# The last two products of a three-stage kernel in thirds of 512 tokens instead of halves of 768

## The chip, the core and the metric

The kernel runs on one core of a Trainium2 chip. The metric is the device time of one execution in microseconds (us). Matrix products run on TensorE (PE; its weight loads are shown apart as PEld), and the other engines are VectorE (DVE), ScalarE (ACT), GpSimd (POOL) and SyncE (SP), which here only issues DMAs. Products are summed in PSUM, which has eight banks of 128 partitions by 512 float32 each.

## What is computed

Three stages follow each other: an attention with a window and block summaries (2 batches, 8 heads, 768 positions, head size 64), a feed-forward layer of width 1024 with a normalisation, and a second feed-forward layer of width 2048. The change is about the last one, and about when its weights are made ready.

```
x = attention(q, k, v)                    # 1536 tokens x 512
h = x @ w_in                              # 1536 x 1024
ln = normalise(h * softmax(h)) * g_ln
x = ln @ w_out                            # 1536 x 512
h = x @ w_in2                             # 1536 x 2048
g = where(h > 0, h, exp(min(h, 0)) - 1)
out = g @ w_out2                          # 1536 x 512
```

## The kernel before

**Three products for one.** Each float32 product of the two feed-forward layers is made of three matmuls (`mm3x`, lines 98 to 100): every operand is split into a rounded part "hi" and the rest "lo", and hi·hi, hi·lo and lo·hi are summed in PSUM. The attention's own small products are plain float32.

**The weights** come as 64-bit floats and are turned into hi and lo on the chip by `convert` (lines 106 to 121), 128x512 words at a time. One conversion is a DMA of 512 KB into a staging slot, ACT's absolute value (L113), POOL's clamp (L114), three DVE steps on the bits (L115, L116, L117), ACT's copy that rounds to hi (L120) and DVE's subtraction that leaves lo (L95). A slot is free again once L117 has read it. There are 48 conversions: 8 of w_in, 8 of w_out, 16 of w_in2 (called w3) and 16 of w_out2 (called w4).

**The first phase** (lines 345 to 433) holds the attention, the first layer and w_in and w_out's conversions. It runs in ticks of one 128-token tile and half a product each. Its last part, after the ticks, holds the rest of the first layer's second product (`y_ps`), whose result goes to the tiles `y`, here two of 768 tokens each.

**The tiles `y` lend their space** until the results come: their rows hold the values that `sum_v` adds up (six DMAs of 128x512), and their 1024-word pieces are the staging slots. With two tiles there are three slots in each: `early` is the six of both, `stage[1]` serves the first w3 weights and `stage[0]`, with one tile of its own, the rest, once `split_y` has turned y[0] into hi and lo (`y_hl`).

**The second phase** (lines 436 to 500) takes the tokens in two halves of TC = 768. For each of the 16 pieces f of the hidden width, `ffn2_in` makes h in two matmul groups of 384 columns (2 x 12 matmuls; tiles h, then m, then the hi and lo of g in `g_hl`): ACT's relu and exp (L447, L448), a DVE step (L449), ACT's copy to hi (L450) and DVE's subtraction to lo (L95). `ffn2_out` then adds piece f into six output sums `o_ps` of 128 tokens each (6 x 3 matmuls of 512 columns). Four of these sums have banks of their own (`pso`), and two take half of the four banks (`psb`) that h is written to. `more_w(2)` at each f converts two more weights while any are left; six w3 and w4 are converted or under way before the second phase begins.

**What sets the order.** SP's DMAs keep the order of the program. The instructions of the other engines are put in an order, engine by engine, by a scheduler when the kernel is built, and each engine then runs its own list strictly in that order (TensorE's is by hand in the last two pieces).

Of the kernel before, what the change touches and what calls it, by code (L numbers as in the profile page):

```python
# [9 lines left out]
F32 = mybir.dt.float32  # L10
# [19 lines left out]
NTOK = B * S  # L30
NJ = NTOK // 128
TB = 384
TC = 768
KD, KF1, KF2 = DM // 128, F1 // 128, F2 // 128
NEG = -1.0e9
LEAD = 6
NBUF = 3
NG = 4


def f32_of(bits):
# [8 lines left out]
def tile_kernel(ctx: ExitStack, tc: tile.TileContext, qd, kT, v, w_in, w_out, g_ln, w_in2, w_out2,  # L50
# [46 lines left out]
    def mm3x(ps, l, ls, r, rs, first, last):  # L97
        nc.tensor.matmul(ps, lhsT=l[0][ls], rhs=r[0][rs], start=first, stop=False)  # L98
        nc.tensor.matmul(ps, lhsT=l[0][ls], rhs=r[1][rs], start=False, stop=False)  # L99
        nc.tensor.matmul(ps, lhsT=l[1][ls], rhs=r[0][rs], start=False, stop=last)  # L100
# [19 lines left out]
        nc.scalar.activation(hi, x, AF.Copy)  # L120
        lo_of(lo, x, hi)

    early = stage[0] + stage[1]

    def load_w_in(n, k):
        cs = slice(n * 512, (n + 1) * 512)
# [22 lines left out]
    def sum_v(b):  # L149
        pst = psb.tile([128, DM], F32, tag="b", name="vs_ps")  # L150
        for i in range(S // 128):
            vt = rows[1][i]
            nc.sync.dma_start(vt, v[b, PAD + i * 128:PAD + (i + 1) * 128, :])
            c0 = NB - i * 4
            nc.tensor.matmul(pst, lhsT=avg[:, c0:c0 + 128], rhs=vt, start=i == 0, stop=i == S // 128 - 1)
        vsum[b] = p_at.tile([128, DM], F32, tag="vsum", name="vsum", bufs=1)
        nc.scalar.activation(vsum[b][WIN:KW, :], pst[WIN:KW, :], AF.Copy)
# [102 lines left out]
    def ffn1_out(i, d, k):  # L260
        if k == 0:
            ys[d] = psb.tile([128, 512], F32, tag="b", name="y_ps")
        mm3x(ys[d][:, :TB], w_out_hl[k], (al, slice(d * 128, (d + 1) * 128)), lnT_of(i), (al, k, al),
             k == 0, k == KF1 - 1)
        if k == KF1 - 1:
            nc.scalar.activation(y[i // 2][:, d, i % 2 * TB:(i % 2 + 1) * TB], ys[d][:, :TB], AF.Copy)

    w3, w4, yhl = [], [], {}

    def bits():  # L270
        state["late"] += 1
        if not yhl:
            return stage[1][state["late"] % 3]
        i = state["late"] % 4
        return stage[0][i] if i < 3 else p_w3.tile([128, KD, 256], I32, name="bits", tag="bits", bufs=1)

    def load_w3():
        f = len(w3)
# [31 lines left out]
            elif len(w4) < KF2:  # L310
                load_w4()

    def split_y(i, n):
        yhl[i, n] = [p_y.tile([128, KD, TB], F32R, tag=f"y{n}{c}", name="y_hl", bufs=1) for c in range(2)]
        for k in range(0, KD, 2):
            src = y[i][:, k:k + 2, n * TB:(n + 1) * TB]
            hi, lo = (t[:, k:k + 2, :] for t in yhl[i, n])
            nc.scalar.activation(hi, src, AF.Copy)
            lo_of(lo, src, hi)

# [70 lines left out]
    for t, (j, n) in enumerate(ticks):  # L391
        s_n, p_n, x_n = t + LEAD, t + LEAD - 2, t + LEAD - 3
        if t == 0:
            sum_v(1)
        elif t == 1:
            load_k(1)
        elif t == 3:
            sum_k(1)
        if x_n < NU and t:
            load_v(x_n)  # L400
        if s_n < NU:
            for u in (s_n + 1, s_n):
                if u < NU and u not in q_bd:
                    load_q(u)
            attn_s(s_n)
        mm_in(j, n)
        if p_n < NU:
            attn_p(p_n)
        for f, *args in after[t]:
            f(*args)  # L410
        if x_n < NU:
            attn_x(x_n)
        more(converts.get(t, 0))
        if t in (13, 15):
            load_w3()
        if x_n == NU - 1:
            p_at.release()
            p_w3 = ctx.enter_context(tc.tile_pool(name="p_w3", bufs=1, side="left", reuse_waits="tile"))
            lnT_last = [p_w3.tile([128, KF1, TB], F32R, tag=f"lnT{c}", name="lnT") for c in range(2)]
    p_in.release()  # L420
    p_y = ctx.enter_context(tc.tile_pool(name="p_y", bufs=1, side="right", reuse_waits="tile"))
    for d in range(KD):
        mm_out(NJ // 3 - 2, d)
        if d == 2:
            split_y(0, 0)
            split_y(0, 1)
        if d < 3:
            tr(NJ - 3 + d)
    for d in range(KD):
# [8 lines left out]
    ghl = [p_w.tile([128, NG, TC], F32R, tag=f"lnT{c}", name="g_hl") for c in range(2)]  # L438

    def ffn2_in(i, f):  # L440
        for n in range(TC // TB):
            gh, gl = (a[:, f % NG, n * TB:(n + 1) * TB] for a in ghl)
            m = p_y.tile([128, TB], F32, tag="m", name="m", bufs=3)
            h2 = psb.tile([128, 512], F32, tag="b", name="h2")[:, :TB]
            for k in range(KD):
                mm3x(h2, w3[f], (al, k, al), yhl[i, n], (al, k, al), k == 0, k == KD - 1)
            nc.scalar.activation(m, h2, AF.Relu, scale=-1.0)  # L447
            nc.scalar.activation(m, m, AF.Exp, scale=-1.0)  # L448
            nc.vector.scalar_tensor_tensor(m, m, -1.0, h2, op0=ALU.add, op1=ALU.max)  # L449
            nc.scalar.activation(gh, m, AF.Copy)  # L450
            lo_of(gl, m, gh)
            if f == KF2 - 1 and i + 1 < NTOK // TC:
                split_y(i + 1, n)

    def ffn2_out(ops, t, f):
        mm3x(ops[t], [a[:, f % NG, :] for a in ghl], (al, slice(t * 128, (t + 1) * 128)), w4[f], (al,),
# [18 lines left out]
        nc.sync.dma_start(out[r0:r0 + 128, :], o)  # L475

    for i in range(NTOK // TC):
        ops = [(pso if t < 4 else psb).tile([128, DM], F32, tag="o" if t < 4 else "b", name="o_ps")
               for t in range(NTT)]
        end = i == NTOK // TC - 1  # L480

        for f in range(KF2 - 2 if end else KF2):
# [71 lines left out]
```

## Time and profile before

| | us |
|---|---|
| median of 3 runs | 505.76 (505.55 to 505.81) |
| the profiled execution | 510.05 |
| its span, first to last instruction | 508.3 |
| TensorE busy in the span | 482.9 (95%) |
| DVE busy | 292.2 (57%) |
| ACT busy | 269.9 (53%) |

The profiled execution is 4.29 us above the median of the runs, and 1.75 us of it lie outside the span. Matmuls are pipelined: a matmul's record is longer than the step from its start to the next one's start, so a product is costed by the starts of a long row of matmuls and not by the mean length of one. The same holds, less strongly, for DVE and ACT. "Idle before" names the engine or DMA that ended a wait.

### The profile page before, as it was taken

The numbers are of one execution on the slowest core, as the hardware profiler recorded it, in microseconds if no ns is written. First come the engines' busy times: TensorE is split into PE (matmuls) and PEld (weight loads), VectorE is DVE, ScalarE is ACT, GpSimd is POOL, SyncE is SP. The second block draws the span as 40 slices with busy tenths as digits, with TensorE's granted clock in tenths as the row PEclk, the third lists the DMA queues.
The fourth block names the chain that finished last, engine by engine and source line by source line (L and its number), as shares of the span: only waits on it lengthen the run. The fifth ranks groups of instructions, "written<-read, shape, count | busy, mean of one in ns | idle before, by whom it ended". The sixth has DMA issues, their size and how long they took to land.

```text
span 508.3 us, 7746 instructions
## 1 busy us (share of the span) xinstructions
PE 482.9 (95%) x2808; PEld 425.3 (84%) x2808; DVE 292.2 (57%) x714; ACT 269.9 (53%) x634; POOL 136.3 (27%) x216
## 2 busy tenths in 40 slices
PE   0888999899999999999999999999999999999997
PEld 0564877688888898999889999999998999999895
DVE  2688899697557126899999982222542323232331
ACT  1674898685657235766777763424452424242441
POOL 1877579589323111322132600000000000000000
PEclk9989999999999999999999999999999999999999
DMA  8967662261301010556455500000030000000003
GB/s 289 334 216 278 204 217 92 77 212 59 114 17 33 17 41 1 166 171 202 142 190 165 166 0 2 1 1 0 1 124 1 0 1 0 1 0 1 1 1 125
DMA packets 24567, 46.58 MB, mean 92 GB/s; under 512 B 2256, under 2 KB 11088, under 8 KB 24528
## 3 DMA queue, kind: packets, MB, share of 16 engines
q1 hardware_dynamic: 24528, 46.08, 28.1%
q8 instruction: 22, 0.36, 0.3%
q14 instruction: 17, 0.14, 0.1%
HBM read 42.93 MB, written 3.15 MB: 91 GB/s over the span
## 4 chain that ended last, share of the span: by engine, by line
PE 72%; DVE 12%; DMA 8%; ACT 3%; issue 2%; SPq 1%; POOL 1%; ACTq 0%; DVEq 0%
PE h L98 11%; PE h L100 11%; PE h L99 11%; PE o_ps L100 9%; PE o_ps L98 9%; PE o_ps L99 9%; DMA y<-in_w_out 4%; PE s_ps L178 3%; DVE conv L116 3%; DMA q_bd<-in_qd 3%; PE y_ps L98 2%; PE y_ps L100 2%; DVE conv L117 2%; PE y_ps L99 2%; PE x_ps L214 2%
## 5 line engine op out<-in xcount | busy, mean ns | idle before, releaser
L449 DVE SCALAR_TENSOR_TENSOR m<-m,h 128x384 f32<-128x384 f32 x64 | 35.2, 551 | 100.6 <-ACT m L448 100.6
L98 PE MATMUL h<-y_hl,w 128*128 128x384 f32 x256 | 86.2, 337 | 0.0
L100 PE MATMUL h<-y_hl,w 128*128 128x384 f32 x256 | 86.2, 337 | 0.0
L99 PE MATMUL h<-y_hl,w 128*128 128x384 f32 x256 | 86.2, 337 | 0.0
L447 ACT ACTIVATE m<-h 128x384 f32<-128x384 f32 x64 | 31.2, 487 | 84.4 <-PE h L100 84.3
L98 PE MATMUL o_ps<-w,g_hl 128*128 128x512 f32 x192 | 75.5, 393 | 0.1
L99 PE MATMUL o_ps<-w,g_hl 128*128 128x512 f32 x192 | 75.3, 392 | 0.0
L100 PE MATMUL o_ps<-w,g_hl 128*128 128x512 f32 x192 | 74.0, 392 | 0.0
L114 POOL TENSOR_SCALAR conv<-conv 128x512 f32<-128x512 f32 x48 | 38.2, 798 | 70.8 <-ACT conv L113 69.6
L192 POOL TENSOR_SCALAR sm<-sm,st 128x120 f32<-128x120 f32 x96 | 47.9, 518 | 23.1 <-DVE st L190 20.7
L95 DVE TENSOR_TENSOR g_hl<-m,g_hl 128x384 fp32r<-128x384 f32 x64 | 37.1, 580 | 27.3 <-ACT g_hl L450 27.2
L450 ACT ACTIVATE g_hl<-m 128x384 fp32r<-128x384 f32 x64 | 33.5, 524 | 33.9 <-DVE m L449 33.9
L99 PEld LDWEIGHTS h<-y_hl,w 128*128 128x128 f32 x256 | 48.0, 188 | 1.6
L98 PEld LDWEIGHTS h<-y_hl,w 128*128 128x128 f32 x256 | 48.0, 187 | 1.6
L100 PEld LDWEIGHTS h<-y_hl,w 128*128 128x128 f32 x256 | 48.0, 187 | 0.1
L178 PE MATMUL s_ps<-kw,q_bd 128*128 128x120 f32 x192 | 29.6, 301 | 15.5 <-DMA q_bd<-in_qd 14.0
L113 ACT ACTIVATE conv<-y 128x512 f32<-128x512 f32 x40 | 27.2, 679 | 32.1 <-DMA y<-in_w_in 11.4
L98 PE MATMUL y_ps<-lnT,w_out 128*128 128x384 f32 x128 | 43.8, 342 | 0.0
L99 PE MATMUL y_ps<-lnT,w_out 128*128 128x384 f32 x128 | 43.1, 337 | 0.0
L100 PE MATMUL y_ps<-lnT,w_out 128*128 128x384 f32 x128 | 42.8, 337 | 0.0
L100 PEld LDWEIGHTS o_ps<-w,g_hl 128*128 128x128 f32 x192 | 36.0, 188 | 7.8
L98 PEld LDWEIGHTS o_ps<-w,g_hl 128*128 128x128 f32 x192 | 36.0, 188 | 7.0 <-ACT g_hl L450 0.5
(77 smaller groups left out, 924.6 us busy)
## 6 DMA issues: line engine op xcount, KB each, us to landing
y<-in_w_out SPq DMA_DIRECT2D x23, 512.0 KB, 3.8
y<-in_w_in SPq DMA_DIRECT2D x17, 512.0 KB, 5.5
q_bd<-in_qd SPq DMA_DIRECT2D x24, 256.0 KB, 4.9
vw<-in_v SPq DMA_DIRECT2D x24, 192.0 KB, 4.1
bits<-in_w_in SPq DMA_DIRECT2D x7, 512.0 KB, 3.7
k_sb<-in_kT SPq DMA_DIRECT2D x8, 400.0 KB, 5.7
y<-in_v SPq DMA_DIRECT2D x12, 256.0 KB, 4.4
out<-y SPq DMA_DIRECT2D x11, 256.0 KB, 2.3
```

The costliest lines, as they stand in the source:

```text
L95: nc.vector.tensor_tensor(out_, x, hi.bitcast(F32), op=ALU.subtract)
L98: nc.tensor.matmul(ps, lhsT=l[0][ls], rhs=r[0][rs], start=first, stop=False)
L99: nc.tensor.matmul(ps, lhsT=l[0][ls], rhs=r[1][rs], start=False, stop=False)
L100: nc.tensor.matmul(ps, lhsT=l[1][ls], rhs=r[0][rs], start=False, stop=last)
L113: nc.scalar.activation(x, high.bitcast(F32), AF.Abs)
L114: nc.gpsimd.tensor_scalar(x, x, F64_HUGE, F64_TINY, op0=ALU.min, op1=ALU.max)
L116: nc.vector.scalar_tensor_tensor(a, high, -0x40000000, a, op0=ALU.bitwise_and, op1=ALU.bitwise_or)
L178: nc.tensor.matmul(sps[:, p, 0:KW], lhsT=q_bd[n][:, p, :], rhs=kw[:, p, :], start=True, stop=True)
L192: nc.gpsimd.tensor_scalar(sm[:, p, :], sm[:, p, :], ri[:, p:p + 1], 1.0, op0=ALU.mult, op1=ALU.mult)
L447: nc.scalar.activation(m, h2, AF.Relu, scale=-1.0)
L449: nc.vector.scalar_tensor_tensor(m, m, -1.0, h2, op0=ALU.add, op1=ALU.max)
L450: nc.scalar.activation(gh, m, AF.Copy)
```

## The change

The second phase takes the tokens in three thirds of 512. `ffn2_in` makes h in one matmul group of 512 columns. The output sums are four and all lie in banks of their own, so h has the other four banks. `g_hl` holds six pieces f instead of four (in the same space). `split_y` turns a whole third into hi and lo.

With three tiles `y` of 512 tokens there are two slots in each. `early` is again six slots, but the rows that `sum_v` fills now cover slots 2, 3 and 4 instead of 3, 4 and 5. The first w3 weights go through the two slots of `stage[2]`. Eight of them are begun in the ticks 13, 15 and 17 to 22, instead of two in 13 and 15. Later weights take two slots of `stage[0]` and two tiles `bits`, instead of three and one.

```diff
-TC = 768
+TC = 512
-NG = 4
+NG = 6
...
-    early = stage[0] + stage[1]
+    early = stage[0] + stage[1] + stage[2]
+    v_rows = rows[1] + rows[2]
...
-            vt = rows[1][i]
+            vt = v_rows[i]
...
-            nc.scalar.activation(y[i // 2][:, d, i % 2 * TB:(i % 2 + 1) * TB], ys[d][:, :TB], AF.Copy)
+
+            t0 = i * TB
+            while t0 < (i + 1) * TB:
+                t1 = min((t0 // TC + 1) * TC, (i + 1) * TB)
+                nc.scalar.activation(y[t0 // TC][:, d, t0 % TC:t0 % TC + t1 - t0],
+                                     ys[d][:, t0 - i * TB:t1 - i * TB], AF.Copy)
+                t0 = t1
...
         if not yhl:
-            return stage[1][state["late"] % 3]
+            return stage[2][state["late"] % 2]
         i = state["late"] % 4
-        return stage[0][i] if i < 3 else p_w3.tile([128, KD, 256], I32, name="bits", tag="bits", bufs=1)
+        return stage[0][i] if i < 2 else p_y.tile([128, KD, 256], I32, name="bits", tag="bits", bufs=2)
...
-    def split_y(i, n):
-        yhl[i, n] = [p_y.tile([128, KD, TB], F32R, tag=f"y{n}{c}", name="y_hl", bufs=1) for c in range(2)]
+    def split_y(i):
+        yhl[i] = [p_y.tile([128, KD, TC], F32R, tag=f"y{c}", name="y_hl", bufs=1) for c in range(2)]
...
-        if t in (13, 15):
+        if t in (13, 15, 17, 18, 19, 20, 21, 22):
             load_w3()
...
-        for n in range(TC // TB):
-            gh, gl = (a[:, f % NG, n * TB:(n + 1) * TB] for a in ghl)
-            m = p_y.tile([128, TB], F32, tag="m", name="m", bufs=3)
-            h2 = psb.tile([128, 512], F32, tag="b", name="h2")[:, :TB]
-            for k in range(KD):
-                mm3x(h2, w3[f], (al, k, al), yhl[i, n], (al, k, al), k == 0, k == KD - 1)
...
+        gh, gl = (a[:, f % NG, :] for a in ghl)
+        m = p_y.tile([128, TC], F32, tag="m", name="m", bufs=3)
+        h2 = psb.tile([128, TC], F32, tag="b", name="h2")
+        for k in range(KD):
+            mm3x(h2, w3[f], (al, k, al), yhl[i], (al, k, al), k == 0, k == KD - 1)
...
-        ops = [(pso if t < 4 else psb).tile([128, DM], F32, tag="o" if t < 4 else "b", name="o_ps")
-               for t in range(NTT)]
+        ops = [pso.tile([128, DM], F32, tag="o", name="o_ps") for t in range(NTT)]
```

**Where instructions move.** The order is shown at three places. In the names, y_65 is y[0], y_66 is y[1] and y_67 is y[2]; a name w with a number is a weight's hi or lo; conv is the tile that a conversion works in.

SP in the first 30 us, where weights and the values for the first `sum_v` are fetched, before:

```order
L153 DMA y_66<-in_v 128x512 x6
L107 DMA y_65<-in_w_in 128x1024
L107 DMA y_66<-in_w_in 128x1024
L161 DMA q_bd<-in_qd 128x512
L165 DMA vw_102<-in_v 96x512
...
L107 DMA y_66<-in_w_in 128x1024 x2
L107 DMA y_65<-in_w_in 128x1024
```

and in the change:

```order
L154 DMA y_66<-in_v 128x512 x4
L154 DMA y_67<-in_v 128x512 x2
L107 DMA y_66<-in_w_in 128x1024 x2
L162 DMA q_bd<-in_qd 128x512
L166 DMA vw_103<-in_v 96x512
...
L107 DMA y_67<-in_w_in 128x1024 x2
L107 DMA y_65<-in_w_in 128x1024
```

Both of the two w_in loads behind the six value loads now go to rows that the values have just filled, where before the first went to a slot that no value touches.

DVE at the first pieces of the second phase, from the first m on, before:

```order
L449 SCALAR_TENSOR_TENSOR m<-m,h_2524 128x384
L115 TENSOR_SCALAR conv<-conv 128x512
L116 SCALAR_TENSOR_TENSOR conv<-bits,conv 128x512
L95 TENSOR_TENSOR w_2722<-conv,w_2722 128x512
L449 SCALAR_TENSOR_TENSOR m<-m,h_2543 128x384
L117 SCALAR_TENSOR_TENSOR conv<-bits,conv 128x512
L95 TENSOR_TENSOR g_hl<-m,g_hl 128x384
L115 TENSOR_SCALAR conv<-conv 128x512
L449 SCALAR_TENSOR_TENSOR m<-m,h_2582 128x384
```

and in the change:

```order
L454 SCALAR_TENSOR_TENSOR m<-m,h_2584 128x512
L115 TENSOR_SCALAR conv<-conv 128x512
L95 TENSOR_TENSOR w_2663<-conv,w_2663 128x512
L116 SCALAR_TENSOR_TENSOR conv<-bits,conv 128x512
L95 TENSOR_TENSOR g_hl<-m,g_hl 128x512
L117 SCALAR_TENSOR_TENSOR conv<-bits,conv 128x512
L115 TENSOR_SCALAR conv<-conv 128x512
L454 SCALAR_TENSOR_TENSOR m<-m,h_2624 128x512
```

From the first m to the g of piece 8 the change has, on DVE, the rows of 14 conversions (the subtraction of the last one just behind) and nine m and nine g of 512 columns.

TensorE at the third output piece (f = 2), before:

```order
L98 MATMUL o_ps<-w_2480,g_hl 128x512
L100 MATMUL o_ps<-w_2480,g_hl 128x512 x2
L98 MATMUL h_2677<-y_hl,w_2_2372 128x384
L99 MATMUL h_2677<-y_hl,w_2_2372 128x384
L100 MATMUL h_2677<-y_hl,w_2_2372 128x384
```

and in the change:

```order
L98 MATMUL o_ps<-w_2504,g_hl 128x512
L99 MATMUL o_ps<-w_2504,g_hl 128x512
L98 MATMUL h_2778<-y_hl,w_2_1897 128x512
L100 MATMUL o_ps<-w_2504,g_hl 128x512 x4
L99 MATMUL h_2778<-y_hl,w_2_1897 128x512
L100 MATMUL h_2778<-y_hl,w_2_1897 128x512
```

The eight matmuls of an output piece that need only g's hi stand first, and the four that need its lo behind them. In the change the h of the pieces 0 to 2 and nine of the 12 matmuls of piece 3 stand ahead of the first output matmul. Ahead of the first L100 of the output pieces 4, 7 and 8 stand 137, 204 and 230 matmuls of the second phase.

## Rows read from the trace of the kernel before

**Rows 1.** The page: busy time, share of the span, instructions of each engine.

```profile
PE 482.9 (95%) x2808; PEld 425.3 (84%) x2808; DVE 292.2 (57%) x714; ACT 269.9 (53%) x634; POOL 136.3 (27%) x216
```

**Rows 2.** Busy time by stretches, in us (instructions), clock, DMA share, GB/s.

```profile
core 0: us, PE busy (x) PEld busy (x) DVE busy (x) ACT busy (x) POOL busy (x), PEclk, DMA share, GB/s
...
240.00:260.00 20.00, 19.93 (x102) 17.95 (x102) 19.90 (x36) 15.27 (x31) 4.41 (x6) 1.00 0.56 177
...
300.00:320.00 20.00, 20.00 (x104) 18.39 (x103) 7.09 (x13) 7.96 (x16) 0.00 (x0) 1.00 0.00 1
```

**Rows 3.** TensorE in order of time: start, length, instruction; ends of rows of matmuls.

```profile
55.40 0.39 PE L98 MATMUL h<-w_in,xT 128*128 128x512 f32 x1
...
59.53 0.39 PE L98 MATMUL h<-w_in,xT 128*128 128x512 f32 x1
...
404.51 0.40 PE L98 MATMUL o_ps<-w,g_hl 128*128 128x512 f32 x1
...
408.72 0.34 PE L98 MATMUL h<-y_hl,w 128*128 128x384 f32 x1
...
475.47 0.34 PE L98 MATMUL h<-y_hl,w 128*128 128x384 f32 x1
...
479.67 0.40 PE L98 MATMUL o_ps<-w,g_hl 128*128 128x512 f32 x1
...
483.76 0.34 PE L98 MATMUL h<-y_hl,w 128*128 128x384 f32 x1
```

**Rows 4.** TensorE in order of time: the second phase's first matmul.

```profile
237.00 0.33 PE L98 MATMUL h<-y_hl,w 128*128 128x384 f32 x1
```

**Rows 5.** DVE by line and shape, 222 to 298 us: count, busy, mean ns.

```profile
L95 DVE TENSOR_TENSOR w<-conv,w 128x512 fp32r<-128x512 f32 x25 | 17.0, 680 | 0.0
L116 DVE SCALAR_TENSOR_TENSOR conv<-y,conv 128x512 int32<-128x512 int32 x18 | 14.0, 777 | 0.2
L117 DVE SCALAR_TENSOR_TENSOR conv<-y,conv 128x512 int32<-128x512 int32 x19 | 13.8, 728 | 0.1
L115 DVE TENSOR_SCALAR conv<-conv 128x512 int32<-128x512 int32 x24 | 12.6, 527 | 0.5 <-POOL conv L114 0.5
L95 DVE TENSOR_TENSOR g_hl<-m,g_hl 128x384 fp32r<-128x384 f32 x14 | 9.2, 660 | 0.0
L449 DVE SCALAR_TENSOR_TENSOR m<-m,h 128x384 f32<-128x384 f32 x15 | 8.1, 541 | 0.0
```

**Rows 6.** DVE in order of time: two L115, three conversions apart, none waiting.

```profile
232.69 0.42 DVE L115 TENSOR_SCALAR conv<-conv 128x512 int32<-128x512 int32 x1
...
240.38 0.42 DVE L115 TENSOR_SCALAR conv<-conv 128x512 int32<-128x512 int32 x1
```

**Rows 7.** ACT and DVE by line and shape, from 200 us on: count, busy, mean ns.

```profile
L448 ACT ACTIVATE m<-m 128x384 f32<-128x384 f32 x64 | 33.6, 524 | 1.8
...
L447 ACT ACTIVATE m<-h 128x384 f32<-128x384 f32 x64 | 31.2, 487 | 84.4 <-PE h L100 84.3
...
L95 DVE TENSOR_TENSOR y_hl<-y,y_hl 128x768 fp32r<-128x768 f32 x8 | 7.2, 954 | 4.7 <-ACT y_hl L318 4.7
L318 ACT ACTIVATE y_hl<-y 128x768 fp32r<-128x768 f32 x8 | 6.2, 835 | 0.3 <-PE h L100 0.3
```

**Rows 8.** SP's DMA issues in the first 60 us (a length includes waits inside).

```profile
13.22 4.26 SPq L107 DMA_DIRECT2D y<-in_w_in  x2
17.52 0.43 SPq L161 DMA_DIRECT2D q_bd<-in_qd  x1
...
33.00 8.69 SPq L153 DMA_DIRECT2D y<-in_v  x6
```

**Rows 9.** TensorE in the first 60 us: two waits for q_bd.

```profile
24.47 1.20 PE L178 MATMUL s_ps<-kw,q_bd 128*128 128x120 f32 x8 [1.23 <-DMA q_bd<-in_qd]
...
46.90 1.12 PE L178 MATMUL s_ps<-kw,q_bd 128*128 128x120 f32 x8 [1.10 <-DMA q_bd<-in_qd]
```

**Rows 10.** DVE in the first 60 us: the slots of w_in's loads 4 and 5 read.

```profile
36.93 0.73 DVE L117 SCALAR_TENSOR_TENSOR conv<-y,conv 128x512 int32<-128x512 int32 x1
...
39.84 0.98 DVE L117 SCALAR_TENSOR_TENSOR conv<-y,conv 128x512 int32<-128x512 int32 x1
```

More of the change, by code (lines that the diff above doesn't have):

```diff
@@ L311, in more_w @@
                 load_w4()
-    def split_y(i, n):
-        yhl[i, n] = [p_y.tile([128, KD, TB], F32R, tag=f"y{n}{c}", name="y_hl", bufs=1) for c in range(2)]
+    def split_y(i):
+        yhl[i] = [p_y.tile([128, KD, TC], F32R, tag=f"y{c}", name="y_hl", bufs=1) for c in range(2)]
         for k in range(0, KD, 2):
-            src = y[i][:, k:k + 2, n * TB:(n + 1) * TB]
-            hi, lo = (t[:, k:k + 2, :] for t in yhl[i, n])
+            src = y[i][:, k:k + 2, :]
+            hi, lo = (t[:, k:k + 2, :] for t in yhl[i])
             nc.scalar.activation(hi, src, AF.Copy)
@@ L424, in tile_kernel @@
         if d == 2:
-            split_y(0, 0)
-            split_y(0, 1)
+            split_y(0)
         if d < 3:
@@ L440, in ffn2_in @@
     def ffn2_in(i, f):
-        for n in range(TC // TB):
-            gh, gl = (a[:, f % NG, n * TB:(n + 1) * TB] for a in ghl)
-            m = p_y.tile([128, TB], F32, tag="m", name="m", bufs=3)
-            h2 = psb.tile([128, 512], F32, tag="b", name="h2")[:, :TB]
-            for k in range(KD):
-                mm3x(h2, w3[f], (al, k, al), yhl[i, n], (al, k, al), k == 0, k == KD - 1)
[L447 to L453, printed above, removed]
+        gh, gl = (a[:, f % NG, :] for a in ghl)
[3 more added lines that the diff above has]
+            mm3x(h2, w3[f], (al, k, al), yhl[i], (al, k, al), k == 0, k == KD - 1)
+        nc.scalar.activation(m, h2, AF.Relu, scale=-1.0)
+        nc.scalar.activation(m, m, AF.Exp, scale=-1.0)
+        nc.vector.scalar_tensor_tensor(m, m, -1.0, h2, op0=ALU.add, op1=ALU.max)
+        nc.scalar.activation(gh, m, AF.Copy)
+        lo_of(gl, m, gh)
+        if f == KF2 - 1 and i + 1 < NTOK // TC:
+            split_y(i + 1)
     def ffn2_out(ops, t, f):
```

## The prediction, made before the changed kernel ran

> **What bounds the kernel now.** The page comes first: TensorE is busy for 482.9 of 508.3 us, far above DVE and ACT [rows 1]. A share of the whole can hide stages, so the stretches come next. In 240 to 260 us TensorE and DVE are both full (19.93 and 19.90 us of 20), in 300 to 320 us TensorE is full and DVE is at 7.09 us; the granted clock is 1.00 in both [rows 2]. The chain of waits names DVE's conversions ahead of the first output matmul, but there the two engines run side by side, and TensorE does not wait. So the second phase lasts as long as its matmuls' steps take, provided that DVE keeps up in its first 60 us. The third thing to read is therefore the step of a matmul, from starts in order of time, since records overlap: 24 matmuls of 384 columns from 475.47 to 479.67 step by 175.0 ns; 18 of 512 columns from 479.67 to 483.76 step by 227.2 ns, and 18 others from 404.51 to 408.72 by 233.9 ns; 18 of w_in with 512 columns (55.40 to 59.53) by 229.4 ns [rows 3].
>
> **The wider first product.** Before, h takes 2 halves x 16 pieces x 24 = 768 matmuls of 384 columns. Now it takes 3 x 16 x 12 = 576 of 512. The columns are the same (294,912), so what can be saved is only what a matmul costs apart from its columns, 192 times. Between 175.0 ns at 384 and 227.2 to 233.9 ns at 512 lie 52.2 to 58.9 ns for 128 columns. If the step is a fixed part and a part for each column, the fixed part is 18.4 ns at one end and nothing at the other. Before: 768 x 175.0 = 134.4 us. Now, by the fastest row, 576 x 227.2 = 130.9 (a gain of 3.5); by the slowest, 134.7 (a loss of 0.3); by w_in's row 576 x 229.4 = 132.1, a gain of 2.3 us. I take 2.5 us (229 ns): w_in's matmuls are the only first product with 512 columns, and more output rows look like the fast one than like the slow one, which I find only at the first pieces of each half.
>
> [...]
>
> **The output product** stays at 576 matmuls of 512 columns: 2 x 16 x 18 before, 3 x 16 x 12 now. Nothing is gained or lost. Four sums in banks of their own leave h four banks; before, TensorE showed no wait for banks in this phase, so that is worth nothing by itself.
>
> **The conversions** are 48 as before, and 12 instead of six are under way when the second phase begins. The six that move cost about 2.56 us of DVE each (three in 232.69 to 240.38 [rows 6]), 15 us in ticks where DVE is idle more than half of the time; TensorE's work hides them. What is left is 20 conversions in a first third of 16 x 24 x 0.229 = 88 us, where before 26 had a first half of 16 x (24 x 0.175 + 18 x 0.229) = 133 us. So DVE has less to do and less time for it, and that is the place that can turn the sign. I walk it by the order. The second phase begins at 237.0 [rows 4]. The first h is summed after 12 x 0.229 = 2.7 us; relu and exp of 512 columns take (487 + 524) x 4/3 = 1.35 us [rows 7]; so DVE can start its first m at 241.1. Ten conversions stand ahead of it instead of 12, so DVE is there in time. From there to the g of piece 8 it has 14 conversions, nine m and nine g. A conversion is 2.56 us [rows 6]. An m of 384 columns shows 0.541 and a g 0.660 [rows 5]; at 512 they lie between that and 4/3 of it, and a subtraction of 512 columns shows 0.680; I take 0.65 and 0.72. Then g of piece 8 is ready at 241.1 + 14 x 2.56 + 9 x 1.37 = 289.3. TensorE reaches the first matmul that wants it after 230 matmuls, at 237.0 + 230 x 0.229 = 289.7. For piece 7 the same sum is 282.8 against 283.7 (204 matmuls), for piece 4 it is 265.9 against 268.4 (137). So DVE is in time by 0.4 to 2.5 us, and I take nothing for it.
>
> Both bounds: in 240 to 260 us DVE got through 36 instructions in 20 us, 0.556 each [rows 2]. The 74 of this stretch would take 41.1 us at that step, and 44 with the wider m and g: 4 us of slack. At the mean records (0.680 + 0.777 + 0.728 + 0.527 = 2.71 us a conversion, m and g at 4/3 [rows 5]) they take 52.3 us and piece 8 is 3.7 us late. This term is 0 to +3.7 us; the step in order of time is nearest to what DVE did, since neighbouring records overlap, and by it the term is 0.
>
> **The change of thirds.** The next third's first h needs `y_hl`, which may be overwritten only when the last h of the old third is summed. TensorE then has 12 output matmuls, 2.75 us. ACT's relu and its first copy (0.487 x 4/3 + 0.835 x 4/3 = 1.76 us) and DVE's first subtraction (0.954 x 4/3 = 1.27) take 3.0 us [rows 7]; what needs the subtraction stands three matmuls further, at 3.4 us. Two changes of thirds cost nothing; with tens of percent more on ACT or DVE they cost up to 0.5 us each. The last lot of output has four sums instead of six to cover the last g: 15 matmuls, 3.4 us, against relu, exp, m and the hi copy of about 2.8 us. Nothing again. The stores and the tail after the last matmul are the same.
>
> **The head.** Two w_in loads follow the six loads of values. Before, the first goes out at once and the second waits for TensorE to have summed two rows; both and the next q_bd are out at 17.52 [rows 8]. In the change both wait, and the second for two rows more, about 1.8 us. TensorE waits there for q_bd already (1.23 us at 24.47 [rows 9]), so 0 to 1.8 us are lost. In return the second six loads of values, out at 33.00 to 41.69 [rows 8], wait for the slots of w_in's loads 2 to 4 instead of 3 to 5. Slot 4 is read at 36.93, slot 5 at 39.84 to 40.82 [rows 10], so SP comes free some 3 us earlier, and the wait of 1.10 us at 46.90 [rows 9] can go. I take 0, with 1.8 us to either side at most.
>
> **Sum.** -2.5 + 0 + 0 + 0 = -2.5 us: the profiled execution of 510.05 would be 507.55. The runs' median lies 4.29 us below it, and I carry that over: 505.76 - 2.5 = 503.3.
>
> **Rivals.**
>
> *Only columns cost.* If the 384-column step of 175.0 ns is 0.456 ns for each column and nothing else (the slow output row has 0.457), 576 matmuls take what 768 took: gain 0, time 505.8. For it: the slow row. Against it: the fast row and w_in's, which are shorter per column than the 384-column one. [...] Chance 17%.
>
> *DVE comes late in the first third* and TensorE waits for g: the end on the other side. Place: pieces 5 to 8. Price: what DVE needs beyond 0.4 us of slack. At the mean records it is 3.7 us late, and the time is 505.76 - 2.5 + 3.7 = 507.0. It eats the gain from 2.5 us of lateness on, when a conversion steps at 2.76 us instead of 2.56. For it: DVE is full there already, and POOL's clamps can hold DVE up. Against it: two conversions fewer ahead of the first m. Chance 12%, and 7% more that it is late by 1 to 3 us and the time is 504.5 to 506.5.
>
> *The head loses its 1.8 us* and gets nothing back: 505.1. For it: TensorE waits for that very DMA. Against: SP is free earlier right after. Chance 8%.
>
> **Chances.** The forecast has 56%. A measurement of this kernel can tell about 0.2% (1.0 us) from no change. Faster by more than that, under 504.75, holds nearly all of the forecast and a part of the small lateness: 0.58. Within 0.2%: only columns, the head and the rest of the lateness, 0.29. Slower: 0.13. The forecast's own range is 501.5 to 504.7 (the fast row and a head that gains 0.8; half of the gain lost). To leave out no more than 2 in 10, the range goes up past the rivals of no change to 506.3 and leaves out the late DVE and the rarest gains: 501.3 to 506.3.
>
> **What the changed profile would show.** The step of h in rows of matmuls: 227 to 230 ns confirms the first term, 233 ns or more the rival of columns. TensorE's starts between 237 and 295 us: no gap over 0.3 us, or else waits of the output matmuls for g at pieces 5 to 8. The first matmul of the second phase at 237 plus or minus 1.8 us tells the head. At the changes of thirds no wait of h for `y_hl`. A second phase that is shorter by 2.5 us while the first phase has moved by more than 1.8 us would mean that the order of the first 100 us matters more than I think.

## The result, and the profile after

The changed kernel took 510.28 us (median; 507.90 to 511.01) against 505.76 (505.55 to 505.86), a ratio of 1.0075 with a 95% interval of 1.0049 to 1.0100. Forecast were 503.3 us and a range of 501.3 to 506.3. In a second comparison, with more executions of both, it was 509.95 against 506.44, a ratio of 1.0054 (1.0031 to 1.0078; the quotient of the two medians is 1.0069). Single executions of the kernel before spread from 504.4 to 509.4 there.

The page of the profiled execution (507.90 us, span 505.8): busy time of each engine. It answers to [rows 1].

```profile
PE 483.2 (96%) x2616; PEld 400.5 (79%) x2616; DVE 283.5 (56%) x680; ACT 261.8 (52%) x592; POOL 131.0 (26%) x216
```

There are 192 matmuls fewer, and TensorE is busy for just as long. Its starts in order of time (start, length, instruction) answer to [rows 3, 4]: the second phase's first h, and the first and the 29th of a row of h.

```profile
234.80 0.39 PE L98 MATMUL h<-y_hl,w 128*128 128x512 f32 x1
...
410.90 0.39 PE L99 MATMUL h<-y_hl,w 128*128 128x512 f32 x1
...
417.43 0.39 PE L99 MATMUL h<-y_hl,w 128*128 128x512 f32 x1
```

28 steps take 6.53 us, 233.2 ns each. The mean over all rows of h is 233.2 as well, so h takes 576 x 0.2332 = 134.3 us, where 768 steps of 0.1751 (the mean before) took 134.5. The predicted gain is not there. Busy time by stretches, as in [rows 2] (the columns are in its first row):

```profile
240.00:260.00 20.00, 20.00 (x87) 16.09 (x86) 19.91 (x33) 14.16 (x25) 4.84 (x7) 1.00 0.49 157
260.00:280.00 20.00, 20.00 (x88) 16.17 (x87) 19.49 (x34) 13.46 (x23) 6.95 (x7) 1.00 0.47 132
280.00:300.00 20.00, 20.00 (x88) 16.28 (x87) 8.88 (x15) 8.40 (x14) 0.58 (x1) 1.00 0.00 1
```

DVE is full until 280 us, but TensorE never waits for it here. From 140 us to the end all its waits together are 0.2 us, and the changes of thirds show none. So the second phase is as long as before (267.4 us from the first h to the end of the last matmul, 267.2 in a repeated profile of before), and what was lost was lost ahead of it. SP and TensorE in the first 40 us, answering to [rows 8, 9]:

```profile
16.35 2.04 SPq L107 DMA_DIRECT2D y<-in_w_in  x2
18.43 0.43 SPq L162 DMA_DIRECT2D q_bd<-in_qd  x1
28.29 0.85 SPq L154 DMA_DIRECT2D y<-in_v  x2
32.79 5.48 SPq L154 DMA_DIRECT2D y<-in_v  x4
38.32 0.90 SPq L162 DMA_DIRECT2D q_bd<-in_qd  x2
```

```profile
24.26 2.03 PE L179 MATMUL s_ps<-kw,q_bd 128*128 128x120 f32 x8 [2.45 <-DMA q_bd<-in_qd]
```

Beside [rows 8, 9] this looks hardly later. That is deceptive: the profiled execution of before was itself a late one, as its repeat shows next.

### The profile page after: what moved, and what is told of

Read it like the earlier page. It is cut to its first block, busy times and chain, and to the rows that moved or that the text cites. A ratio compares the mean times of both kernels' runs of the same rounds, so it can differ in the third digit from the quotient of the medians.

```text
span 505.8 us, 7269 instructions
## 1 busy us (share of the span) xinstructions
PE 483.2 (96%) x2616; PEld 400.5 (79%) x2616; DVE 283.5 (56%) x680; ACT 261.8 (52%) x592; POOL 131.0 (26%) x216
## 4 chain that ended last, share of the span: by engine, by line
PE 88%; DMA 3%; DVE 3%; ACT 2%; POOL 1%; issue 1%; SPq 1%; ACTq 0%; POOLq 0%
PE h L98 13%; PE h L100 13%; PE h L99 13%; PE o_ps L98 9%; PE o_ps L99 9%; PE o_ps L100 9%; PE y_ps L98 5%; PE y_ps L100 4%; PE s_ps L179 4%; PE y_ps L99 4%; PE x_ps L215 2%; DMA q_bd<-in_qd 2%; PE p_ps L198 2%; PE t_ps L254 1%; DMA k_sb<-in_kT 1%
## 5 line engine op out<-in xcount | busy, mean ns | idle before, releaser
L454 DVE SCALAR_TENSOR_TENSOR m<-m,h 128x512 f32<-128x512 f32 x48 | 32.9, 685 | 120.0 <-ACT m L453 119.8
L452 ACT ACTIVATE m<-h 128x512 f32<-128x512 f32 x48 | 28.7, 598 | 107.5 <-PE h L100 107.2
L99 PE MATMUL h<-y_hl,w 128*128 128x512 f32 x192 | 75.9, 395 | 0.0
L100 PE MATMUL h<-y_hl,w 128*128 128x512 f32 x192 | 75.9, 395 | 0.0
L98 PE MATMUL o_ps<-w,g_hl 128*128 128x512 f32 x192 | 75.5, 393 | 0.0
L99 PE MATMUL o_ps<-w,g_hl 128*128 128x512 f32 x192 | 75.4, 393 | 0.0
L98 PE MATMUL h<-y_hl,w 128*128 128x512 f32 x192 | 75.2, 395 | 0.0
L100 PE MATMUL o_ps<-w,g_hl 128*128 128x512 f32 x192 | 66.9, 392 | 0.0
L114 POOL TENSOR_SCALAR conv<-conv 128x512 f32<-128x512 f32 x48 | 36.4, 761 | 67.2 <-ACT conv L113 65.9
L193 POOL TENSOR_SCALAR sm<-sm,st 128x120 f32<-128x120 f32 x96 | 44.9, 484 | 16.7 <-DVE st L191 15.8
L95 DVE TENSOR_TENSOR g_hl<-m,g_hl 128x512 fp32r<-128x512 f32 x48 | 33.9, 707 | 24.4 <-ACT g_hl L455 24.4
L455 ACT ACTIVATE g_hl<-m 128x512 fp32r<-128x512 f32 x48 | 30.3, 630 | 32.5 <-DVE m L454 32.5
L100 PE MATMUL y_ps<-lnT,w_out 128*128 128x384 f32 x128 | 43.1, 338 | 0.0
L99 PEld LDWEIGHTS h<-y_hl,w 128*128 128x128 f32 x192 | 36.1, 188 | 8.6
L98 PEld LDWEIGHTS o_ps<-w,g_hl 128*128 128x128 f32 x192 | 36.1, 188 | 8.5
L100 PEld LDWEIGHTS h<-y_hl,w 128*128 128x128 f32 x192 | 36.1, 188 | 8.5
L98 PEld LDWEIGHTS h<-y_hl,w 128*128 128x128 f32 x192 | 36.1, 188 | 8.5
L100 PEld LDWEIGHTS o_ps<-w,g_hl 128*128 128x128 f32 x192 | 36.1, 188 | 8.2
L99 PEld LDWEIGHTS o_ps<-w,g_hl 128*128 128x128 f32 x192 | 36.1, 188 | 8.2
```

The costliest lines, as they stand in the source:

```text
L95: nc.vector.tensor_tensor(out_, x, hi.bitcast(F32), op=ALU.subtract)
L114: nc.gpsimd.tensor_scalar(x, x, F64_HUGE, F64_TINY, op0=ALU.min, op1=ALU.max)
L193: nc.gpsimd.tensor_scalar(sm[:, p, :], sm[:, p, :], ri[:, p:p + 1], 1.0, op0=ALU.mult, op1=ALU.mult)
```

## Experiments

### Which rows of y hold the values

Both kernels were run again, with each other's place for sum_v's values. The edit in the change, and its mirror image in the kernel before:

```diff
-    v_rows = rows[1] + rows[2]
+    v_rows = rows[1][2:] + rows[2]     # slots 3 to 5, as before
```

```diff
+    v_rows = rows[0][4:] + rows[1]     # slots 2 to 4, as in the change
...
-            vt = rows[1][i]
+            vt = v_rows[i]
```

> The kernel before, unchanged, for a second trace and the spread of its executions on this chip. Both theories: 505.8 us within 0.3, executions within 0.4 us of each other. Open is its profiled execution: 510 us again would mean that recording costs it 4 us; some 506 us that the first trace was an odd one. The second phase's first matmul is then expected near 233 us instead of 237.0, the step of 384 columns at 175 ns as before.

> The change, unchanged, for the spread of its executions (507.9 to 511.0 so far) and a second trace. Theory H (head): the second phase takes 267 us in every execution, 576 matmuls of h by 233 ns and no gap over 0.3 us, and a slower execution begins its second phase later (234.8 in the first trace; 237 to 238.5 in one of 509 us). Theory T (first third): the second phase's start stays near 234.8 and TensorE waits 1 to 3 us for g between 237 and 295 us.

> The change with one part undone: the values that sum_v adds up lie in the staging slots 3, 4 and 5 as in the kernel before, so the first of the two w_in loads behind them waits for nothing. Theory H: the head is as before, about 505.8 us or up to 1 us less, and executions agree within 0.5 us. Theory T: 510 us with the same spread, since the second phase is untouched.

> The kernel before with one part of the change: the values lie in the slots 2, 3 and 4, so both w_in loads behind them wait. Theory H: 507 to 511 us, with a spread of 2 to 3 us. Theory T: 505.8 us as before, the head's order costs nothing.

| kernel | median, us | ratio to before (95%) | first h of phase 1 | first h of phase 2 |
|---|---|---|---|---|
| before | 506.47 | 0.9995 (0.9972 to 1.0018) | 26.58 | 233.38 |
| before, slots 2 to 4 | 509.38 | 1.0052 (1.0028 to 1.0076) | 31.99 | 236.66 |
| change | 509.95 | 1.0054 (1.0031 to 1.0078) | 31.04 | 235.48 |
| change, slots 3 to 5 | 507.50 | 1.0021 (1.0000 to 1.0042) | 27.05 | 234.62 |

The slots alone cost the kernel before 2.9 us, and undoing them gives the change 2.45 us back. Theory H holds for this part, and T falls. H's own figures were missed in part: the change with slots 3 to 5 was expected at 505.8 us or less with executions within 0.5 us, and takes 506.46 to 508.91. Nor is the spread a matter of the slots: the repeat of before, expected within 0.4 us, spreads from 504.86 to 508.89. How the loss comes about is seen in two profiles of the kernel before that differ in the slots, and in the order that the scheduler made with them. SP's loads and TensorE's third group of s_ps, with the slots of before:

```profile
12.23 0.43 SPq L107 DMA_DIRECT2D y<-in_w_in  x1
...
16.64 0.33 SPq L107 DMA_DIRECT2D y<-in_w_in  x1
17.01 0.43 SPq L161 DMA_DIRECT2D q_bd<-in_qd  x1
```

```profile
22.50 1.12 PE L178 MATMUL s_ps<-kw,q_bd 128*128 128x120 f32 x8 [0.17 <-DMA q_bd<-in_qd]
```

and with the slots of the change, SP, TensorE, and three stretches (PEclk, DMA share and GB/s are the last three columns):

```profile
16.88 2.04 SPq L107 DMA_DIRECT2D y<-in_w_in  x2
18.97 0.43 SPq L162 DMA_DIRECT2D q_bd<-in_qd  x1
```

```profile
26.39 2.03 PE L179 MATMUL s_ps<-kw,q_bd 128*128 128x120 f32 x8 [3.93 <-DMA q_bd<-in_qd]
```

```profile
16.00:18.00 2.00, 2.00 (x6) 0.81 (x6) 1.97 (x4) 1.35 (x8) 1.90 (x3) 1.00 0.43 137
...
26.00:28.00 2.00, 1.61 (x7) 1.64 (x8) 0.00 (x0) 0.26 (x1) 0.53 (x1) 0.50 1.06 296
28.00:30.00 2.00, 2.00 (x32) 1.79 (x33) 1.54 (x10) 0.96 (x4) 0.51 (x1) 0.50 1.02 393
```

Three things follow each other. The first of the two weight loads goes out 4.65 us later, and meanwhile the DMA engines idle (0.43 busy in 16 to 18 us, where the kernel before has 0.98). The query load goes out 2.0 us later, but the wait for it ends 3.9 us later; two loads of 512 KB now stand just ahead of it. And TensorE, which did nothing from 22.46 to 26.39, runs at a granted clock of 0.50 from 26 to 32 us, where the kernel before had 1.00 in this profile. The first h comes 5.4 us later, and 3.3 us of it are left at the second phase; the same pair of profiles of the change has 4.0 and 0.9 us. What becomes of the lateness in between is not shown: with the slots TensorE's order changed too, in 203 places between 37 and 133 us. So the 2.4 to 2.9 us are the price of the slots and of that order together, and what each has in it was not separated.

A version in which no load waits for values puts them in three tiles that are needed later (ln):

```diff
+        vts = [p_ln.tile([128, F1], F32, tag="ln", name="v_ln", bufs=5) for _ in range(3)]
...
-            vt = v_rows[i]
+            vt = vts[i // 2][:, i % 2 * DM:(i % 2 + 1) * DM]
```

> The change, with the values of sum_v in three tiles of their own (the later ln tiles) instead of rows of y: no w_in load waits for the sums of values, and no load of values waits for a w_in slot. Theory H (the change loses time because w_in's third load goes out some 4 us later, and the query load behind it lands late): the third group of s_ps starts by 22.8 us, the wait for its q_bd is under 0.5 us (3.9 us in the change), the first h of the first phase starts by 27.2 us, and the time is 505.5 to 507.5 (0.9975 to 1.0005 of the change with the slots of before). Rival D (the DMA engines are full in 10 to 30 us, so an earlier load only pushes others back): the first h starts at 29 us or later and the time stays at 508 to 510. The tiles of w4's pieces 0 to 4 also come to lie at a multiple of 64 bytes here (32 beside one before): if that is what makes their output steps slow (233 to 235 ns), these fall to 228 to 230 ns; if not, they stay.

> The kernel before with the values of sum_v in three tiles of their own. Theory H: the second of the two w_in loads goes out at about 12.7 us instead of 16.64, the third group of s_ps starts at 22.5 us or earlier, and the later wait of the second values for slots is gone as well: 504.0 to 506.0, equal to the kernel before or up to 2 us below it. Rival D: 506 to 508, because the same bytes come in the same time.

The change with it took 507.76 us (1.0018, 1.0003 to 1.0033), the kernel before 505.85 (0.9992, 0.9975 to 1.0009). In the change the third group of s_ps starts at 22.80 without a wait for q_bd and the first h at 27.21, as H said, so D falls. But the time is no better than with the slots of before, and a little above the range given. A row of 36 output matmuls of w4's first pieces steps by 229.5 ns, where the change has 234.0. So without any wait in the head about 1 us of the loss is still there.

### What a matmul's step depends on

h in two groups of 256 columns, to separate columns from a fixed part:

```diff
-        for k in range(KD):
-            mm3x(h2, w3[f], (al, k, al), yhl[i], (al, k, al), k == 0, k == KD - 1)
+        for cs in (slice(0, TC // 2), slice(TC // 2, TC)):
+            for k in range(KD):
+                mm3x(h2[:, cs], w3[f], (al, k, al), yhl[i], (al, k, cs), k == 0, k == KD - 1)
```

> The change with h made in two groups of 256 columns instead of one of 512: 1152 matmuls instead of 576, the same columns. Theory C (columns alone, 233.2 ns at 512 and 175.1 at 384): the step is 116.5 to 117.5 ns, and the second phase is as long as in the change, 267 us within 1. Theory F (a fixed part of 10 to 18 ns for each matmul, which the predicted gain rested on): 121 to 126 ns, and the second phase is 5 to 11 us longer.

The mean step is 116.4 ns. 23 steps of a slower row in its profile, 117.8 ns each:

```profile
465.32 0.28 PE L98 MATMUL h<-y_hl,w 128*128 128x256 f32 x1
...
468.03 0.28 PE L100 MATMUL h<-y_hl,w 128*128 128x256 f32 x1
```

116.4, 175.1 and 233.2 ns at 256, 384 and 512 columns are 0.455, 0.456 and 0.455 ns a column: theory C, for these operands in these places (it had named 116.5 to 117.5). (One execution: 507.11 us.) The other explanation of 233 against the 227 of other rows was the place. In the built program w3's tiles start at 0x080 modulo 512 bytes of a partition, the operand y_hl that streams past them at 0x140; g_hl and the pieces 8 to 15 of w4, whose output rows are fast, both start at 0x140; w4's pieces 0 to 4 start at 0x1E0 and 5 to 7 at 0x080. So 192 bytes were put ahead of everything on the left side of the memory, on top of the values apart:

```diff
+    com.tile([128, 48], F32, name="pad0")
     ident = com.tile([128, 128], F32, name="ident")
```

> The change with the values apart and 192 bytes of padding ahead of all tiles on the left side, so that the weights w3 of the first product lie at 0x140 modulo 512 like the weights of the products that step fast. Theory P (the place of the weights makes the step of h 233 ns where the output's last rows step by 227): h steps by 227 to 229 ns and the time is 2.3 to 3.4 us below the kernel with the values apart. Theory C (a matmul here costs its columns alone, about 0.455 ns each for this product): h stays at 232.5 to 234 ns and the time is equal within 0.5 us.

It took 502.66 us, 0.9922 (0.9902 to 0.9942) of before, 5.1 below the kernel without the padding. A row of 29 h without it, and with it:

```profile
410.89 0.39 PE L99 MATMUL h<-y_hl,w 128*128 128x512 f32 x1
...
417.42 0.39 PE L99 MATMUL h<-y_hl,w 128*128 128x512 f32 x1
```

```profile
408.27 0.39 PE L100 MATMUL h<-y_hl,w 128*128 128x512 f32 x1
...
414.62 0.39 PE L100 MATMUL h<-y_hl,w 128*128 128x512 f32 x1
```

233.2 against 226.8 ns. The mean of all h is 227.6, and the output's mean goes from 229.8 to 227.7 since w4's pieces 5 to 7 move along: 576 x (5.6 + 2.1) ns = 4.4 us of the 5.1. Next, the same padding alone in the kernel before:

> The kernel before with the 192 bytes of padding and nothing else, so that w3 lies at 0x140 modulo 512 there too, with h in 384 columns. Theory W (a place off a multiple of 128 bytes takes some 3% off every matmul of the product, whatever its width): the step of h falls from 175 to about 170 ns, and the time by 3 to 4.5 us, to about 502: then 512 columns are worth nothing, and the place is all. Theory F (at 384 columns a part of the step does not depend on the columns, and hides behind the slow place): h stays at 174 to 175 ns and the time within 1 us of before: then 512 columns are worth some 3.5 us, but only with the weights so placed.

```profile
455.08 0.33 PE L99 MATMUL h<-y_hl,w 128*128 128x384 f32 x1
...
459.09 0.33 PE L101 MATMUL h<-y_hl,w 128*128 128x384 f32 x1
```

It took 506.55 us (1.0005, 0.9984 to 1.0026), and the mean step is 174.5 ns instead of 175.1. Theory F: at 384 columns the place hardly matters. So in good places 512 columns are worth 768 x 174.5 - 576 x 226.7 = 3.4 us, and in the change's places nothing. (In this kernel w4's pieces 0 to 4 still lie at 0x1E0; the h of the pieces 10 to 15, which stand beside other outputs, has 174.5 ns too.)

Four more kernels asked which places are good. In all of them the values are apart. The first pads w3's tiles apart, so that the pieces lie at seven places (its pads are left out below); the second moves y_hl to w3's 0x080 (192 bytes behind y_hl, in a pool that grows downwards); the third pads by 448 bytes instead of 192; the fourth adds to the 192 bytes a shift of w4's pieces 0 to 4 from 0x180 to 0x140, so that all operands lie alike.

```diff
+        if i == 0:
+            p_y.tile([128, 48], F32, name="pad0")     # second: y_hl at 0x080
...
+    com.tile([128, 112], F32, name="pad0")            # third: w3 at 0x040
...
+    p_ln.tile([128, 112], F32, name="pad1")           # fourth: ahead of ln, and
+            p_ln.tile([128, 16], F32, name="pad2")    # behind it
```

> The change with the values apart, and paddings that put the weights of the 16 pieces f at different places modulo 512 bytes: 0x100 (f 0), 0x180 (f 1), 0xC0 (f 2 to 7), 0x140 (8 to 10), 0x1C0 (11 to 13), 0x000 (14), 0x0A0 (15). Read are the steps of h by f. Theory G128 (a multiple of 128 bytes is slow, an odd multiple of 64 fast): 233 ns at f 0, 1 and 14, 226 to 228 at 2 to 13. Theory S (the weights must lie like the operand y_hl that streams past them, which is at 0x140 modulo 512): 226 to 228 at 8 to 10 alone, 233 elsewhere. f 15 stands off a multiple of 64, as the slow w4 pieces did: 233 or more.

> The change with the values apart; w3 stays at 0x080 modulo 512, and y_hl is moved from 0x140 to 0x080 by 192 bytes of padding on the other side. Theory S (alike is what counts): h steps by 226 to 229 ns. Theory A (the weights' own place counts): 233 as before the padding.

> The change with the values apart and 448 bytes of padding on the left: w3 at 0x040 modulo 512, y_hl at 0x140, alike modulo 256 but not 512. If likeness modulo 256 counts: 226 to 229 ns; if modulo 512: 230 to 233.

> The kernel with the values apart and the 192 bytes, and besides w4's pieces 0 to 4 moved to 0x140 modulo 512, where they stood at 0x180: now w3, y_hl, g_hl and all of w4 lie alike. Theory S (a matmul steps fast where its weights and the operand that streams past lie alike modulo 256 or 512, and rows next to slow ones are slow with them): the h of the pieces 4 to 7, which stepped by 228 to 231 ns among output matmuls of 229 to 235, comes down to 226 to 227 like the other pieces, 0.5 to 1.3 us in all. Rival (those pieces are slow for a reason of their own): the steps there stay.

> The kernel with the values apart and the 192 bytes once more, for the comparison on the same chip: 502 to 503.5, 0.990 to 0.994 of before.

| kernel | mean step of h, ns | by pieces | us |
|---|---|---|---|
| several places | 232.0 | 0x0C0, 0x1C0, 0x180, 0x0A0: 232 to 234; 0x000, 0x100: 230 to 231; 0x140: 231, 229, 228 | 505.42, one |
| both at 0x080 | 228.2 | 227 to 228 at 1 to 10, 230 to 231 at 0 and 11 to 15 | 502.88, one |
| 0x040 and 0x140 | 227.6 | 229 to 231 at 4 to 7, 227 to 228 elsewhere | 502.99, one |
| 192 bytes again | 227.6 | as the row above | 502.97 (0.9923, 0.9902 to 0.9944) |
| all alike | 226.7 | 226.7 everywhere but the first | 502.18 (0.9915, 0.9884 to 0.9947) |

Likeness counts in these kernels, not the weights' own place: with both at 0x080 most of h is fast (227 to 228 ns, where 0x080 beside 0x140 had 233.2). Likeness modulo 256 is enough here (227.6 ns at 0x040 and 0x140). "An odd multiple of 64 is fast" falls at 0x0C0 and 0x1C0 (232 to 234 ns). w_in's rows bear it out: their operands lie at 0x140 and 0x040, and from the eighth matmul of a row (after 100 us) the mean step is 227.5 ns; with the 192 bytes they lie at 0x140 and 0x100, and it is 229.2. The pieces 4 to 7, which stayed slow with the 192 bytes (229 to 231 ns), came down to 226.7 when w4's first pieces were moved: their h stands behind the unlike outputs of the pieces 1 to 4. The last pieces with both at 0x080 show the same inside a row. Beside them stand outputs whose operands lie at 0x140, alike among themselves but not with 0x080, where the pieces before stand beside w4 at 0x180 and 0x080. A row of 18 such h, its first, 11th and last matmul:

```profile
416.45 0.39 PE L100 MATMUL h<-y_hl,w 128*128 128x512 f32 x1
...
418.76 0.39 PE L98 MATMUL h<-y_hl,w 128*128 128x512 f32 x1
...
420.35 0.39 PE L99 MATMUL h<-y_hl,w 128*128 128x512 f32 x1
```

The first ten steps take 231 ns each, the other seven 227. So a change of places from one row to the next slows the first ten matmuls here, and a row of 12 is over before much is gained. A row of 29 h with all alike, 226.8 ns:

```profile
406.94 0.39 PE L101 MATMUL h<-y_hl,w 128*128 128x512 f32 x1
...
413.29 0.39 PE L101 MATMUL h<-y_hl,w 128*128 128x512 f32 x1
```

Why a step changes by 6.5 ns (233.2 to 226.7) with the distance between the two operands' places is open: the trace doesn't show where the time goes.

### The early conversions

Two early conversions of w3, as before, instead of eight:

```diff
-        if t in (13, 15, 17, 18, 19, 20, 21, 22):
+        if t in (13, 15):
```

> The change with the values apart, and two early conversions of w3 (ticks 13 and 15) instead of eight. Theory of the prediction (DVE keeps up in the first third by 0.4 to 2.5 us of slack because six conversions were moved; each is 2.56 us of DVE): without the move DVE is 6 x 2.56 - 2.5 = about 13 us late at the last, TensorE waits for g in 240 to 310 us, and the time is 515 to 523. Rival: DVE has much more room than that, the waits are under 5 us in all and the time is below 513.

> The change with the values apart and two early conversions, timed (one look gave 507.0). Theory E: 0.5 to 1.5 us below the same kernel with eight. Rival: equal within 0.3 us.

> The change with the values apart and its eight early conversions once more, for the comparison on the same chip: 506.5 to 508.5.

> The kernel with the values apart and all operands alike, and two early conversions of w3 instead of eight. Theory E (an early conversion costs the first phase something, because ACT takes its absolute value, waiting for the transfer, ahead of a copy of lnT for which TensorE waits; and DVE keeps up in the first third without it): the wait of 1.1 us at 158 us is gone, no gap of TensorE over 0.3 us stands between 235 and 300 us, and the time is 0.5 to 1.5 us below the kernel with eight: 500.7 to 501.7. Rival (the shorter steps take DVE's slack, so that TensorE now waits for g): 502 to 506, with waits of the output matmuls at the pieces 4 to 8.

| kernel | eight early, us | two early, us |
|---|---|---|
| change, values apart | 507.63 (1.0013, 0.9996 to 1.0030) | 505.81 (0.9981, 0.9963 to 0.9999) |
| the same, all alike | 502.18 (0.9915, 0.9884 to 0.9947) | 500.54 (0.9879, 0.9854 to 0.9905) |

The first row is one comparison; the two of the second come from two comparisons, each with its own runs of before (506.80 and 506.55). A single execution with two early conversions, values apart, had taken 507.00. Two are better than eight, by 1.6 to 1.8 us. The prediction's 13 us of lateness without the move are not there at all; stretches of the kernel with two, values apart:

```profile
240.00:260.00 20.00, 20.00 (x88) 16.26 (x87) 19.93 (x34) 13.93 (x26) 3.61 (x5) 1.00 0.50 157
260.00:280.00 20.00, 20.00 (x88) 16.21 (x87) 19.86 (x34) 14.15 (x25) 6.78 (x7) 1.00 0.59 170
280.00:300.00 20.00, 20.00 (x88) 16.25 (x88) 16.95 (x30) 12.37 (x22) 3.75 (x5) 1.00 0.21 68
```

From 200 to 320 us DVE is busy for 99.4 us here and for 86.2 with eight, and TensorE waits for nothing from 140 us on. The order was made anew for this kernel: its first output matmul comes at 247.01, 12.36 us after the first h, where with eight it comes after 10.49, and with six pieces in g_hl there is room for h to run ahead. The g of the pieces 4, 7 and 8 are ready 3.0 to 3.7 us before TensorE wants their lo, and 3.7 to 4.1 us in the change. What eight cost shows in the first phase. ACT in order of time, and the TensorE instruction that waits, values apart and eight early conversions:

```profile
157.13 0.68 ACT L113 ACTIVATE conv<-y 128x512 f32<-128x512 f32 x1 [0.72 <-DMA y<-in_w_in]
157.70 0.60 ACT L256 ACTIVATE lnT<-t_ps 128x512 fp32r<-128x512 f32 x1
```

```profile
159.08 0.45 PE L98 MATMUL y_ps<-lnT,w_out 128*128 128x384 f32 x1 [1.07 <-DVE lnT L95]
```

An early conversion's first step waits on ACT for its transfer, and the copy of lnT that TensorE needs is queued behind it. With two there is no such wait. In the change itself this wait is 0.2 us, and 0.3 with the slots of before, but its length is not the whole cost. The change with the slots of before has TensorE's order of the kernel before up to the second phase, and ACT's up to 145 us, where the first differing conversion stands. The same two matmuls in the repeat of before, and in that kernel:

```profile
149.12 0.39 PE L98 MATMUL h<-w_in,xT 128*128 128x512 f32 x1
...
157.38 0.42 PE L98 MATMUL y_ps<-lnT,w_out 128*128 128x384 f32 x1
```

```profile
149.44 0.39 PE L98 MATMUL h<-w_in,xT 128*128 128x512 f32 x1
...
158.59 0.44 PE L98 MATMUL y_ps<-lnT,w_out 128*128 128x384 f32 x1 [0.34 <-DVE lnT L95]
```

8.26 us became 9.15, although ACT's L113 waits for no transfer there. The stretch takes 8.7 to 9.6 us in all twelve profiles of kernels with eight early conversions (8.7 and 8.8 in the change), and 8.26 to 8.28 in all eight with two. So the conversions cost 0.5 us here in the change and 0.9 with the slots of before; of the 1.6 to 1.8 us above it shows 0.6 to 1.3, and where the rest goes is open. The last kernel, with values apart, all operands alike and two early conversions, is the fastest: 1.2% below the kernel before. Its g are ready only 0.5 to 0.9 us ahead of TensorE at the pieces 4, 7 and 8, so DVE has little left to give. Its page:

```profile
PE 476.2 (95%) x2616; PEld 400.2 (80%) x2616; DVE 287.2 (57%) x680; ACT 261.0 (52%) x592; POOL 134.8 (27%) x216
```

## Why the prediction was wrong, by its own steps

**The wider first product** was sized at -2.5 us and measured -0.2. The failing step is the choice of 229 ns by "w_in's matmuls are the only first product with 512 columns". The number of columns was not what set the fast and slow rows of [rows 3] apart. The fast output rows (227.2 ns) have weights and streaming operand alike modulo 256, and so has w_in's product, from which the 229 ns came; the slow ones (w4's pieces 0 to 4, 233.9 ns) don't, and neither do w3 and y_hl (233.2 ns). The rival that only columns cost, at 17%, was what happened to this term, and its test (233 ns or more) told it at once. The other bound, -3.5 us, is what the kernel with all alike reaches (3.4). A fixed part of each matmul, the prediction's reason for a gain, is not shown even so: from 174.5 and 226.7 ns it would be some 18 ns, and 256 columns would step by 122, but they stepped by 116.4 (in the unlike places; alike ones were not tried). The shortest mean step of h at 512 columns in these runs is 226.7 ns.

**The output product**, nothing: right. Its mean step is 230.7 ns, 230.1 to 230.3 before.

**DVE in the first third**, nothing: right, and its 19% for being late were too many. The walk by the order came out with 0.4 to 2.5 us to spare, and 3.7 to 4.1 are there: piece 8's g is ready 49.9 us after the first h, not 52.3. And it took the order as given, but the kernel with two early conversions shows that another order makes room for 13.2 us more of DVE's work between 200 and 320 us. The half-sentence that TensorE's work hides the six moved conversions failed: where lateness was looked for, on DVE, there was none, and what cost was their place in ACT's order ahead of the lnT copies, with or without a wait for the transfer. Every engine that a moved step queues on has to be walked, as was done for SP.

**The change of thirds and the end**, nothing: right.

**The head** was taken at 0 with 1.8 us to either side, and the slots, with the order that came with them, measure +2.4 (in the change) and +2.9 (in the kernel before). The place was right, and three steps of the sum failed. The row of 4.26 us in [rows 8] holds two issues, and the price was worked out for the second; the first load is the one that goes out 4.65 us later. The wait was priced at the issue of q_bd (+2.0, close to the 1.8), not at its landing behind two large loads (+3.9). And the granted clock of 0.50 that was measured behind the wait (26 to 32 us in the kernel before with these slots) was not in the sum, though the profile that the rows come from has 0.50 too, in 26 to 28 us. The gain that was set against it, SP free 3 us earlier, is not there: the q_bd loads behind the second values go out at 38.32, and at 38.89 in the repeat of before.

**The basis.** The rows came from an execution 4.29 us above the median, and the difference was carried over as a constant. It was itself in the first phase: the repeat of before starts the second phase at 233.38, not 237.00 [rows 4], and waits 0.17 us for q_bd at the place where [rows 9] have 1.23. 2.4 us of the gap stand at the first h (29.02 against 26.58), 0.8 at 53 us, and 3.6 at 100 us, so not all of it is the head's. "TensorE waits there already" was read from an untypical execution, and made the loss look as if it were half paid. For the same reason the sign named for the head, the second phase's first matmul at 237 us, misled: it came at 234.80, and the head had lost time.

**The sum** as measured: 0 for the columns, +2.4 for the slots, and about +1 that is left with the slots of before (507.50 against 506.47), of which the profiles show 0.9 at the early conversions; with the values apart they cost 1.8 us. That is +3.5 us, the difference of the medians in the second comparison; its ratio makes it 2.7, and the first comparison has +4.5.

## What to carry to other kernels

A step per matmul is carried from one product to another only after comparing where their weights and streaming operands lie, and those of the rows beside them; a pad of some hundred bytes that makes both alike modulo 256 is a cheap thing to try (here 192 bytes took the step of h from 233.2 to 227.6 ns and the time from 507.76 to 502.66 us), and can decide whether a wider matmul pays. When a buffer is moved, look which load goes out first into the new place and what lands behind it, not only which wait is added, and whether the scheduler's order moved with it. And before rows carry a sum, see whether the profiled execution is a typical one: a gap to the median lies somewhere in the rows.

## What was not expected of the hardware

The step of a 512-column product moves between 226.7 and 234 ns with the places of its two operands alone, and the effect lasts over some ten matmuls of the next row, of another product too (ten steps of 231 ns in a row of h behind output matmuls, then 227); at 384 columns the same shift moves it by less than 1 ns (175.1 to 174.5). And 3.93 us without a matmul ahead of 26.39 us, in the kernel before with the slots of the change, were followed by some 6 us at a granted clock of 0.50, while in the repeat of the kernel before, with its own slots and waits of 0.2 to 0.5 us there, it stayed at 1.00. The first profile of the kernel before, with waits of 0.47, 0.45 and 1.23 us ahead of 24.47, has 0.50 in 26 to 28 us as well.
